# Transposes of q, k and x moved from TensorE to DMA from tile 10 on, with a reordered start and end, in a sliding-window attention and squared-ReLU MLP kernel

## The chip, the cores and the metric

The kernel runs on one core of one Trainium2 chip. The metric is the device time of one execution in microseconds. A core has five engines with in-order instruction streams: TensorE (PE in the profile; its weight loads are listed as PEld), VectorE (DVE), ScalarE (ACT), GpSimd (POOL) and SyncE (SP). SP, ACT and POOL also issue DMAs. An instruction that has to wait holds up everything behind it on its engine.

## The reference

Inputs: q, k, v of shape (4, 8, 768, 64) in fp32 (batch, heads, positions, head size), w_in (512, 2048), w_out (2048, 512); n_global = 8, n_local = 96. Output: (3072, 512) in fp32.

```python
scores = scale * np.matmul(q, k.transpose(0, 1, 3, 2))
rel = pos[:, None] - pos[None, :]
is_global = pos[None, :] < n_global
is_local = (rel >= 0) & (rel < n_local)
dist = np.where(is_global & ~is_local, float(n_local), np.abs(rel))
scores = scores - slopes[:, None, None] * dist          # slopes: one per head
scores = np.where(is_global | is_local, scores, -1e9)
a = softmax(scores)
x = (a @ v).transpose(0, 2, 1, 3).reshape(B * S, H * D)  # (3072, 512)
h = x @ w_in
out = np.maximum(h, 0) ** 2 @ w_out
```

Each position attends to the 96 positions up to itself and to the first 8 positions of its sequence.

## The kernel before

**Tiles and blocks.** The 3072 rows are cut into 24 tiles of 128 (6 for each of 4 batches). A tile goes through attention; two tiles form a block for the MLP, so there are 12 blocks. All matmuls take bf16, except the transposes of tiles 0 and 1, whose q and k come in fp32 by SP and ACT (`plain_q`, `plain_k`, L185). All other loads are issued by POOL (L177) and cast to bf16 on the way.

**Attention of a tile.** PE transposes q and k in four 128x128 blocks each, one per pair of heads (`trq`, `trk`, L327), into PSUM. DVE or ACT copies them out (L264, L266): q into `qz`, in which the two heads of a pair stand in separate halves with zeros between (two copies; the zeros are set at the start, L196), k into `kT`. Four times, once for each pair, PE makes two `sc` matmuls (L375: against the tile's own keys and those of the tile before; the first tile of a batch has only its own), ACT takes exp (L403), and DVE multiplies by `E` (L423), the exponential of mask and slope made once from `pb`. `E0` is the same for the first tile of a batch, where the global keys stand in the tile itself; it is made on ACT from `pb0` (L271). Then in two halves PE multiplies with v (`po`, L466; v has a column of ones, which gives the row sums), and DVE takes the reciprocal and scales into `x` (L491, L492). The first 8 rows of kT and v of each batch are copied into the next tiles (L442, L509), so that two key tiles are enough for each query tile.

**MLP of a block.** PE transposes x (`trx`, L528), a copy puts it into `xT`. Eight steps over d_ff follow: eight `hT` matmuls (L565), relu on ACT (`hr`, L586), square on DVE (`hs`, L598), then two `acc` matmuls (L629) for each of the two row tiles (`sub` 0 and 1), which add up over the eight steps. The sums are copied to `o` and stored by SP (L663).

**What sets the order.** A planner in the kernel (`Plan`) takes the operations with assumed costs, lags and keys, and places at each step the one that can start first, then the one with the lowest key. The result is written out engine by engine; the chip sees only that fixed order and the semaphores. A tile's key lies 12 steps (`LEAD`) ahead of its block's, so attention of later tiles is woven between the MLP steps of earlier blocks. `takes=(ring, n, users)` is a ring of n buffers: `qz` has 4 tiles, `kT` 12, the loaded `q` and `k` 10 each, `x` 2, `xT` 3.

Of the kernel before, what the change touches and what calls it, by code (L numbers as in the profile page):

```python
# [12 lines left out]
FP32 = mybir.dt.float32  # L13
# [84 lines left out]
def kernel(  # L98
# [36 lines left out]
    NQ, NKT, NQZ = 10, 2 * TPB, 4  # L135
# [24 lines left out]
    pb0 = const([P, P], FP32, "pb0")  # L160
    plan = Plan()
    NHS = 14
    LEAD = 12
# [29 lines left out]
    make_identity(nc, ident)  # L193
    nc.vector.tensor_copy(ident32, ident)
    for i in range(NQZ):
        nc.vector.memset(qz[i].bitcast(I32), 0)  # L196
# [12 lines left out]
    nc.vector.tensor_copy(pb0, pb[:, 0, :])  # L209
    nc.vector.tensor_scalar_max(  # L210
        pb0[:n_global, :], pb0[:n_global, :], float(-n_local)
    )
    nc.vector.memset(pb[:n_global, 1, :], float(-n_local))
    for j in range(NT):
        nc.vector.memset(v_sb[j][:, :, D : D + 1], 1.0)  # L215
# [5 lines left out]
    def load_tile(j):  # L221
        q_tile[j], k_tile[j] = q_ring[j % NQ], k_ring[j % NQ]
        for n, dst, src in (("q", q_tile[j], q), ("k", k_tile[j], k)):
# [38 lines left out]
    def any_copy(e, dst, src):  # L262
        if e == "ACT":
            nc.scalar.copy(dst, src)  # L264
        else:
            nc.vector.tensor_copy(dst, src)  # L266

    maskE0 = plan.op(
        ("E0",), {"ACT": 1.6}, key=-99, ready=3.4,
        emit=lambda e: [  # L270
            nc.scalar.activation(E0[:, h // 2, h % 2, :], pb0, Act.Exp, scale=float(slopes[h]))  # L271
            for h in range(H)
        ],
    )
    maskE = [
        plan.op(
            ("E", pair), {"ACT": 0.62}, key=-7 + pair, ready=3.4,
# [9 lines left out]

    tiles = {}
    qz_users = [[] for _ in range(NQZ)]
    kT_users = [[] for _ in range(NKT)]  # L290
    qk_users = [[] for _ in range(NQ)]
    xT_op = {}
# [4 lines left out]
    for j in range(NT):  # L297
# [6 lines left out]
        if j in late:  # L304
            def emit_load(e, j=j):
                load_tile(j)
            ld = plan.op(
                ("load", j), {"POOLQ": 2.6}, emit_load,
                deps=qk_users[j % NQ], key=base, ready=clock[0],
            )  # L310
            qk_users[j % NQ] = []
            land["q", j] = land["k", j] = land["v", j] = ld
# [3 lines left out]
        if True:  # L316
            fp = j < NPLAIN
            parts = []
            for n in ("q", "k"):
                users = []  # L320

                def emit_tr(e, j=j, n=n, fp=fp):
                    pool, tag = (ps_acc, "acc") if fp else (ps_h, "hT")
                    tr = pool.tile([P, NPAIR, P], FP32 if fp else BF16, name=f"tr{n}", tag=tag)
                    src = (q_tile if n == "q" else k_tile)[j]
                    for pair in range(NPAIR):
                        nc.tensor.transpose(  # L327
                            out=tr[:, pair, :], in_=src[:, pair * P : (pair + 1) * P],
                            identity=ident32 if fp else ident,
                        )  # L330
                    tiles["tr", n, j] = tr

                tr = plan.op(
                    ("tr", n, j), {"PE": 0.85 if fp else 0.24}, emit_tr,
                    deps=[land[n, j]], key=base, takes=("acc", NACC, users) if fp else ("hT", 5 - NACC, users),
                )
                users.append(tr)
                if n == "q":
                    for e_ in range(2):
                        half = slice(e_ * D, (e_ + 1) * D)  # L340

                        def emit_z(e, j=j, e_=e_, half=half, zi=zi):
                            any_copy(e, qz[zi][half, :, e_, :], tiles["tr", "q", j][half])

                        z = plan.op(
                            ("z", e_, j), {"DVE": 0.43, "ACT": 0.57}, emit_z,
                            deps=[tr] + qz_users[zi], key=base + 0.1,
                        )
                        users.append(z)
                        parts.append(z)  # L350
                else:
                    def emit_kT(e, j=j, ki=ki):
                        any_copy(e, kT[ki], tiles["tr", "k", j])

                    c = plan.op(
                        ("kT", j), {"DVE": 0.43, "ACT": 0.57}, emit_kT,
                        deps=[tr] + kT_users[ki], key=base + 0.1,
                    )
                    users.append(c)
                    parts.append(c)  # L360
            if not fp:
                qk_users[j % NQ] += [parts[0], parts[-1]]
# [5 lines left out]
        for pair in range(NPAIR):  # L368
            users = []

            def emit_sc(e, j=j, pair=pair, first=first, zi=zi):
                sc = ps_sc.tile([P, 2, 2 * P], FP32, name="sc", tag="sc")
                tiles["sc", j, pair] = sc
                for i in range(1 if first else 2):
                    nc.tensor.matmul(  # L375
                        out=sc[:, i, :],
                        lhsT=kT[(j - i) % NKT][:, pair, :],
                        rhs=qz[zi][:, pair, :, :],
                        start=True,
                        stop=True,  # L380
                        skip_group_check=True,
                    )
# [4 lines left out]
            s_ = plan.op(  # L387
                ("sc", j, pair), {"PE": 0.11 if first else 0.22}, emit_sc, deps=deps,
# [10 lines left out]
            def emit_exp(e, j=j, pair=pair, first=first):  # L399
                n = 2 * P if first else 4 * P  # L400
                esc = work.tile([P, 4 * P], BF16, name="esc", tag="esc", bufs=3)
                sc = tiles.pop(("sc", j, pair))
                nc.scalar.activation(  # L403
                    out=esc[:, :n], in_=sc.rearrange("p a b -> p (a b)")[:, :n],
                    func=Act.Exp, scale=scale,
                )
                tiles["esc", j, pair] = esc

            x_ = plan.op(
                ("exp", j, pair), {"ACT": 0.36 if first else 0.58}, emit_exp, deps=[s_],  # L410
# [6 lines left out]
            def emit_mul(e, j=j, pair=pair, first=first):  # L417
                at = work.tile([P, 4 * P], BF16, name="at", tag="at", bufs=6)
                if first:
                    at_, bias = at[:, : 2 * P], E0[:, pair].rearrange("p b c -> p (b c)")  # L420
                else:
                    at_, bias = at, E[:, pair].rearrange("p i e c -> p (i e c)")
                nc.vector.tensor_mul(  # L423
                    at_, tiles.pop(("esc", j, pair))[:, : at_.shape[1]], bias
                )
                tiles["at", j, pair] = at

            m_ = plan.op(
                ("mul", j, pair), vec(0.24 if first else 0.38), emit_mul,
                deps=[x_, maskE0 if first else maskE[pair]],  # L430
# [4 lines left out]
            mul.append(m_)  # L435
            mul_users.append(musers)
# [18 lines left out]
        for hf in range(2):  # L455
            users = []

            def emit_pv(e, j=j, hf=hf, first=first):
                po = ps_o.tile([P, 4, D + 1], FP32, name="po", tag="po")
                tiles["po", j, hf] = po  # L460
                for hi in range(4):
                    h = 4 * hf + hi
                    at = tiles["at", j, h // 2].rearrange("p (i e c) -> p i e c", i=2, e=2)
                    kjs = (j,) if first else (j, j - 1)
                    for i, kj in enumerate(kjs):
                        nc.tensor.matmul(  # L466
                            out=po[:, hi, :],
                            lhsT=at[:, i, h % 2, :],
# [51 lines left out]
        if True:  # L520
# [26 lines left out]
            xusers.append(f_)  # L547
        xT_op[j] = c
# [64 lines left out]
    for blk in range(NBLK):  # L613
# [7 lines left out]
        for s, sub in order2:  # L621
            users = acc_users[sub]

            def emit_s2(e, blk=blk, s=s, sub=sub):
# [17 lines left out]
                key=8 * blk + s + 2.0, takes=("acc", NACC, users) if s == 0 else None,  # L642
# [3 lines left out]
            if s == NSTEP - 1:  # L646
                ousers = []

                def emit_o(e, blk=blk, sub=sub):
                    o_sb = work.tile([P, d_model], FP32, name="o", tag="o", bufs=4)  # L650
                    any_copy(e, o_sb, tiles.pop(("acc", blk, sub)))
                    tiles["o", blk, sub] = o_sb

                ev = plan.op(
                    ("o", blk, sub), {"ACT": 0.57, "DVE": 0.62}, emit_o,
                    deps=[o], key=8 * blk + s + 1.0, takes=("o", 4, ousers),
                )
                users.append(ev)
                ousers.append(ev)

                def emit_st(e, blk=blk, sub=sub):
                    r0 = (blk * 2 + sub) * P
                    nc.sync.dma_start(out=out[r0 : r0 + P, :], in_=tiles.pop(("o", blk, sub)))  # L663

                st = plan.op(("st", blk, sub), {"SP": 0.4}, emit_st, deps=[ev], key=8 * blk + s + 9.0)
                ousers.append(st)
# [39 lines left out]
```

## Time and profile before

| what | value |
|---|---|
| median of 3 runs (235.57 to 236.24) | 236.1 us |
| profiled execution | 236.87 us |
| its span, first to last instruction | 235.1 us |
| mean granted TensorE clock | 0.997 |
| busy: PE, DVE, ACT, POOL | 93%, 65%, 64%, 31% |
| instructions: PE matmuls, DVE, ACT | 1968, 399, 282 |
| HBM read and written | 27.26 MB and 6.29 MB |

The profile is one execution. Time outside the span (1.77 us) belongs to no instruction. "Busy" is an average over stages that are unlike: a start in which data arrives, a long even middle, and an end in which the last block drains. Rows of groups read: line, engine, operation, out<-in, shapes, count | busy us, mean ns of one | idle time of that engine just before, and what ended it. Rows of the timeline read: start us, length us, engine, line, operation, count, and in brackets the idle time before.

### The profile page before, as it was taken

To read this page: it belongs to the slowest core of one execution; us is meant where nothing else is said; L and a number is where in the kernel's file an instruction comes from. 1 tells how busy PE (TensorE), PEld (TensorE's weight loads), DVE (VectorE), ACT (ScalarE), POOL (GpSimd) and SP (SyncE) were. 2 spreads that over 40 slices of the span, in tenths; PEclk is the share of its full clock that TensorE was granted. 3 is DMA by queue.
4 is the path that set the end of the run, shared out by engine and by line. 5 is a ranking of instruction groups with operands and counts; after the bars stand their busy time and mean duration, and the time that the engine had idled before them with its cause. 6 is when DMAs were issued, how large, how long until landed. Compare 5 with 4: busy or idle time off the path is not lost.

```text
span 235.1 us, 4992 instructions
## 1 busy us (share of the span) xinstructions
PE 219.5 (93%) x1968; PEld 159.1 (68%) x1968; DVE 153.8 (65%) x399; ACT 149.8 (64%) x282; POOL 73.8 (31%) x94
## 2 busy tenths in 40 slices
PE   1768699999999999999999999999999999999992
PEld 1646467866777777777777777777777777776660
DVE  5778466895756866755766766665766676664532
ACT  5778346763686776775776776766776766743341
POOL 6995488797979242143100000000000000000000
PEclk9999999999999999999999999999999999999998
DMA  7999999999999991964900200200200200200202
GB/s 155 138 155 196 180 187 194 157 175 181 203 159 151 193 63 12 156 46 26 158 0 0 92 0 3 89 1 3 89 4 0 92 0 0 92 0 3 89 0 89
DMA packets 84758, 20.76 MB, mean 88 GB/s; under 512 B 75520, under 2 KB 81664, under 8 KB 84736
## 3 DMA queue, kind: packets, MB, share of 16 engines
q0 software_dynamic: 77120, 13.11, 72.0%
q1 hardware_dynamic: 5536, 6.82, 8.4%
q10 hardware_dynamic: 2080, 0.52, 1.2%
q8 instruction: 15, 0.25, 0.4%
q14 instruction: 7, 0.06, 0.1%
HBM read 27.26 MB, written 6.29 MB: 143 GB/s over the span
## 4 chain that ended last, share of the span: by engine, by line
PE 85%; DMA 6%; POOL 3%; DVE 3%; issue 1%; ACT 1%; POOLq 0%
PE hT L565 35%; PE acc L629 33%; PE sc L375 7%; DMA win<-in_moe_w_in_dram 4%; PE po L466 4%; DMA k<-in_k_dram 2%; PE trx L528 2%; PE trk L327 2%; PE trq L327 2%; POOL v L177 2%; DVE qz L196 1%; POOL q L177 1%; DVE x L492 1%; POOL k L177 0%; DVE hs L598 0%
## 5 line engine op out<-in xcount | busy, mean ns | idle before, releaser
L629 PE MATMUL acc<-wout,hs 128*128 128x512 bf16 x384 | 101.1, 379 | 0.8 <-DVE hs L598 0.8
L565 PE MATMUL hT<-xT,win 128*128 128x256 bf16 x768 | 98.4, 273 | 1.9 <-DMA win<-in_moe_w_in_dram 1.9
L586 ACT ACTIVATE hr<-hT 128x512 f32<-128x512 f32 x96 | 57.4, 598 | 62.9 <-PE hT L565 62.6
L565 PEld LDWEIGHTS <-win 128*128 128x128 bf16 x768 | 74.0, 98 | 24.0 <-DMA win<-in_moe_w_in_dram 2.9
L598 DVE TENSOR_TENSOR hs<-hr 128x512 bf16<-128x512 f32 x96 | 65.6, 683 | 27.2 <-ACT hr L586 27.0
L403 ACT ACTIVATE esc<-sc 128x512 bf16<-128x512 f32 (+1 forms) x96 | 52.8, 558 | 5.0 <-PE sc L375 4.4
L629 PEld LDWEIGHTS <-hs 128*128 128x128 bf16 x384 | 34.0, 98 | 21.6 <-DVE hs L598 1.4
L423 DVE TENSOR_TENSOR at<-esc,E 128x512 bf16<-128x512 bf16 (+1 forms) x96 | 37.4, 392 | 0.5 <-ACT esc L403 0.3
L375 PE MATMUL sc<-qz,kT 128*128 128x256 bf16 x176 | 34.5, 277 | 0.2
L177 POOL DMA_DIRECT2D q<-in_q_dram x22 | 19.8, 899 | 28.2 <-PE trk L327 24.3
L491 DVE RECIPROCAL rs<-po 128x4 f32<-128x4 f32 x48 | 8.7, 181 | 30.2 <-PE po L466 29.8
L177 POOL DMA_DIRECT2D v<-in_v_dram x24 | 21.8, 908 | 3.6 <-DVE v L215 1.5
L492 DVE TENSOR_TENSOR x<-po,rs 128x256 bf16<-128x256 f32 x48 | 20.4, 424 | 1.7
L375 PEld LDWEIGHTS <-kT 128*128 128x128 bf16 x176 | 16.9, 99 | 6.0 <-issue 0.3
L177 POOL DMA_DIRECT2D k<-in_k_dram x22 | 19.7, 897 | 2.0 <-DMA q<-in_q_dram 1.0
L466 PE MATMUL po<-v,at 128*128 128x65 bf16 x352 | 19.0, 194 | 1.1 <-DVE x L492 1.1
L466 PEld LDWEIGHTS <-at 128*128 128x128 bf16 x352 | 17.0, 98 | 4.0 <-DVE x L492 1.5
L264 ACT COPY qz<-trq 64x512 bf16<-64x512 bf16 x23 | 13.3, 580 | 5.1 <-DVE qz L266 2.9
L266 DVE COPY qz<-trq 64x512 bf16<-64x512 bf16 x21 | 8.8, 418 | 6.7 <-PE trq L327 5.8
L264 ACT COPY kT<-trk 128x512 bf16<-128x512 bf16 x20 | 11.7, 586 | 1.2 <-PE trk L327 0.7
L264 ACT COPY xT<-trx 128x512 bf16<-128x512 bf16 x17 | 10.0, 589 | 1.3 <-PE trx L528 1.0
L528 PEld LDWEIGHTS <-x 128*128 128x128 bf16 x96 | 7.3, 98 | 4.9 <-DVE x L492 0.4
(39 smaller groups left out, 103.1 us busy)
## 6 DMA issues: line engine op xcount, KB each, us to landing
out_dram<-o SPq DMA_DIRECT2D x24, 256.0 KB, 2.2
v<-in_v_dram POOLq DMA_DIRECT2D x24, 128.0 KB, 6.5
q<-in_q_dram POOLq DMA_DIRECT2D x22, 128.0 KB, 6.4
k<-in_k_dram POOLq DMA_DIRECT2D x22, 128.0 KB, 6.6
win<-in_moe_w_in_dram POOLq DMA_DIRECT2D x8, 256.0 KB, 8.8
wout<-in_moe_w_out_dram POOLq DMA_DIRECT2D x8, 256.0 KB, 8.8
plain_k<-in_k_dram ACTq DMA_DIRECT2D x2, 256.0 KB, 5.4
plain_q<-in_q_dram SPq DMA_DIRECT2D x2, 256.0 KB, 5.0
```

Source lines behind the costliest of these rows:

```text
L177: nc.gpsimd.dma_start(out=dst, in_=src)
L264: nc.scalar.copy(dst, src)
L375: nc.tensor.matmul(out=sc[:, i, :], lhsT=kT[(j - i) % NKT][:, pair, :], rhs=qz[zi][:, pair, :, :], start=True, stop=True, skip_group_check ...
L403: nc.scalar.activation(out=esc[:, :n], in_=sc.rearrange("p a b -> p (a b)")[:, :n], func=Act.Exp, scale=scale,)
L423: nc.vector.tensor_mul(at_, tiles.pop(("esc", j, pair))[:, : at_.shape[1]], bias)
L466: nc.tensor.matmul(out=po[:, hi, :], lhsT=at[:, i, h % 2, :], rhs=v_sb[kj][:, h, :], start=(i == 0), stop=(i == len(kjs) - 1), skip_group_ ...
L492: nc.vector.tensor_tensor(out=x[:, 4 * hf : 4 * hf + 4, :], in0=po[:, :, :D], in1=rs.to_broadcast([P, 4, D]), op=Alu.mult,)
L528: nc.tensor.transpose(out=trx[:, kt, :], in_=x[:, kt * P : (kt + 1) * P], identity=ident)
L565: nc.tensor.matmul(out=hT[:, c, :], lhsT=w_in_sb[s][:, kt, c * P : (c + 1) * P], rhs=tiles["xT", blk][:, kt, :], start=(kt == 0), stop=(kt ...
L586: nc.scalar.activation(hr, tiles.pop(("hT", blk, s)), Act.Relu)
L598: nc.vector.tensor_mul(hs, hr, hr)
L629: nc.tensor.matmul(out=tiles["acc", blk, sub], lhsT=hs[:, c, sub * P : (sub + 1) * P], rhs=w_out_sb[s][:, c, :], start=(s == 0 and c == 0) ...
```

## The change

- From tile 10 on (`JQK`), q and k are no longer transposed on PE. q is loaded by two DMAs (one for the even heads, one for the odd) into `q_pad`, a ring of 8 tiles that already has the zeros between the heads; SP then issues two DMA transposes, `q_pad` to `qz` and `k` to `kT` (operation "T"). POOL zeroes the 8 `q_pad` tiles ahead of tile 10's load.
- From tile 10 on (`JX`), x is transposed by one DMA transpose that SP issues, straight into `xT`.
- Eight matmuls of a tile of zeros stand ahead of the first transpose on PE.
- The ones in v are set ahead of the `qz` zeros on DVE; two of the four `qz` fills come after the mask.
- `E0` is made on DVE from `E`: a copy of its first half, and for the 8 global rows the larger of its two halves.
- In the first tile of a batch, two pairs share one `sc` tile, one exp and one multiplication.
- In the last block, `sub` 1's acc matmuls have a key 50 higher than `sub` 0's, and its last copy and store are made in two halves of 256 columns, one copied by ACT, one by DVE.
- Some of the planner's costs and earliest times (`HOLD`) are changed.

```diff
+    JQK, JX = 10, 10
+    NQ, NPAD, NKT, NQZ = 10, 8, 2 * TPB, 4
+    q_pad = [const([P, NPAIR, 2, P], BF16, f"qpad_{i}") for i in range(NPAD)]
+    NWARM = 8
+    HOLD = {2: 12.5, 3: 15.0}
 make_identity(nc, ident)
+    nc.vector.memset(zero.bitcast(I32), 0)
+    for j in range(NT):
+        nc.vector.memset(v_sb[j][:, :, D : D + 1], 1.0)
...
+    warm = ps_o.tile([P, 4 * P], FP32, name="warm", tag="po")
+    for i in range(NWARM):
+        nc.tensor.matmul(out=warm, lhsT=zero[:, :P], rhs=zero, start=True, stop=True)
...
     def load_tile(j):
+        k_tile[j] = k_ring[j % NQ]
+        todo = [("k", k_tile[j], k)]
+        if j < JQK:
+            q_tile[j] = q_ring[j % NQ]
+            todo.insert(0, ("q", q_tile[j], q))
+        else:
+            q_tile[j] = q_pad[j % NPAD]
+            s_ = src_rows(q, j).rearrange("(a e) p d -> e p a d", e=2)
+            for e in range(2):
+                swdge(("q", j), q_tile[j][:, :, e, e * D : (e + 1) * D], s_[e], 0.43)
...
-    maskE0 = plan.op(
-        ("E0",), {"ACT": 1.6}, key=-99, ready=3.4,
...
+    def emit_E0(e, c):
+        pairs = slice(2 * c, 2 * c + 2)
+        nc.vector.tensor_copy(E0[:, pairs], E[:, pairs, 0])
+        nc.vector.tensor_max(
+            E0[:n_global, pairs], E[:n_global, pairs, 0], E[:n_global, pairs, 1]
+        )
...
             def emit_load(e, j=j):
+                if j == JQK:
+                    for i in range(NPAD):
+                        nc.gpsimd.memset(q_pad[i].bitcast(I32), 0)
                 load_tile(j)
...
+        if j >= JQK:
+            def emit_dT(e, j=j, zi=zi, ki=ki):
+                nc.sync.dma_start_transpose(
+                    out=qz[zi].rearrange("p a b c -> p (a b) c"),
+                    in_=q_tile[j].rearrange("p a b c -> p (a b c)"),
+                )
+                nc.sync.dma_start_transpose(out=kT[ki], in_=k_tile[j])
+            T = plan.op(
+                ("T", j), {"SP": 2.7}, emit_dT,
+                deps=[land["q", j], land["k", j]] + qz_users[zi] + kT_users[ki],
+                key=base - 6,
+            )
...
-        if True:
+        if j < JX:
             users = []
             def emit_f(e, j=j):
...
+        else:
+            def emit_xT(e, j=j, blk=blk, tt=tt):
...
+                nc.sync.dma_start_transpose(
+                    out=tiles["xT", blk][:, :, tt * P : (tt + 1) * P],
+                    in_=tiles["x", j].rearrange("p h d -> p (h d)"),
+                )
+            c = plan.op(("xT", j), {"SP": 1.3}, emit_xT, deps=norm, key=base + 5, takes=xT_ring)
...
-                key=8 * blk + s + 2.0, takes=("acc", NACC, users) if s == 0 else None,
+                key=8 * blk + s + 2.0 + (50 if last and sub else 0),
+                takes=("acc", NACC, users) if s == 0 else None,
...
+                for half in (0, 1) if last and sub == 1 else (None,):
```

How the order changes, at three places. First SP. Before, its whole program is two loads and the 24 stores:

```order
L701 UNCONDITIONAL_BRANCH
L185 DMA plain_q_157<-in_q_dram 128x8x64
L185 DMA plain_q_161<-in_q_dram 128x8x64
L663 DMA out_dram<-o 128x512 x24
L701 UNCONDITIONAL_BRANCH
```

In the changed kernel, from the stores of block 2 on (the number behind qz or kT is its buffer; the first two rows are tile 13's T operation, and the first xT row is tile 10's):

```order
L397 DMA_TRANSPOSE qz_140<-qpad_90 128x8x128
L401 DMA_TRANSPOSE kT_128<-k_96 128x4x128
L397 DMA_TRANSPOSE qz_141<-qpad_91 128x8x128
L401 DMA_TRANSPOSE kT_129<-k_97 128x4x128
L600 DMA_TRANSPOSE xT<-x 128x4x128
L733 DMA out_dram<-o 128x512 x2
L397 DMA_TRANSPOSE qz_142<-qpad_92 128x8x128
L401 DMA_TRANSPOSE kT_130<-k_98 128x4x128
```

Now 42 transposes share SP's stream with the stores: each tile's x stands behind the T operation of a tile four or more later, and two tiles' x and T stand between the stores of two blocks.

Second the end of PE's stream. Before, from the last hT group on, each row standing for a pair of matmuls (acc_3651 is `sub` 0, acc_3657 `sub` 1; the number behind wout is one more than the 143 of step 0 for each step):

```order
L565 MATMUL hT_3734<-xT_3438,win_7_142 128x256
L629 MATMUL acc_3651<-wout_6_149,hs_3730 128x512
L629 MATMUL acc_3657<-wout_6_149,hs_3730 128x512
L629 MATMUL acc_3651<-wout_7_150,hs_3749 128x512
L629 MATMUL acc_3657<-wout_7_150,hs_3749 128x512
```

In the changed kernel (acc_3420 is `sub` 0, acc_3502 `sub` 1; `sub` 1's steps 3 to 7 follow the last row):

```order
L624 MATMUL hT_3487<-xT_3207,win_7_150 128x256
L688 MATMUL acc_3420<-wout_5_156,hs_3481 128x512
L688 MATMUL acc_3502<-wout_0_151,hs_3405 128x512
L688 MATMUL acc_3420<-wout_6_157,hs_3496 128x512
L688 MATMUL acc_3502<-wout_1_152,hs_3423 128x512
L688 MATMUL acc_3502<-wout_2_153,hs_3436 128x512
L688 MATMUL acc_3420<-wout_7_158,hs_3507 128x512
```

`sub` 1's eight steps have moved behind the last hT; before they went step by step with `sub` 0's.

Third the start of DVE's stream, ahead of the first copy from PSUM. Before:

```order
L194 CAST ident_152<-ident 128x128
L196 MEMSET qz_131 128x512
L196 MEMSET qz_132 128x512
L196 MEMSET qz_133 128x512
L196 MEMSET qz_134 128x512
L209 COPY pb_156<-pb 128x128
L210 TENSOR_SCALAR pb_156<-pb_156 8x128
L213 MEMSET pb 8x128
L215 MEMSET v_95 128x8
```

In the changed kernel, from the last of the 24 fills of v on (the zero tile and the other 23 stand ahead):

```order
L200 MEMSET v_126 128x8
L201 CAST ident_160<-ident 128x128
L202 MEMSET qz_139 128x512
L203 MEMSET qz_140 128x512
L216 MEMSET pb 8x128
L217 MEMSET qz_141 128x512
L218 MEMSET qz_142 128x512
```

V's fills, which stood last, now stand first, behind the zero tile alone; the two instructions on pb0 are gone.

More of the change, by code (lines that the diff above doesn't have):

```diff
@@ L286 @@
     ]
+    def emit_E0(e, c):
[4 more added lines that the diff above has]
+        )
+    maskE0 = [
+        plan.op(
+            ("E0", c), {"DVE": 0.6}, emit=lambda e, c=c: emit_E0(e, c), key=-9 + c,
+            deps=maskE[2 * c : 2 * c + 2],
+        )
+        for c in range(2)
+    ]
     tiles = {}
@@ L291 @@
     qk_users = [[] for _ in range(NQ)]
+    pad_users = [[] for _ in range(NPAD)]
     xT_op = {}
@@ L308 @@
                 ("load", j), {"POOLQ": 2.6}, emit_load,
-                deps=qk_users[j % NQ], key=base, ready=clock[0],
+                deps=qk_users[j % NQ] + (pad_users[j % NPAD] if j >= JQK else []),
+                key=base, ready=clock[0],
             )
             qk_users[j % NQ] = []
+            if j >= JQK:
+                pad_users[j % NPAD] = []
             land["q", j] = land["k", j] = land["v", j] = ld
         zi, ki = j % NQZ, j % NKT
-        if True:
[L317 to L335, printed above, removed]
-                )
[L337 to L360, printed above, removed]
-            if not fp:
-                qk_users[j % NQ] += [parts[0], parts[-1]]
@@ new lines, with emit_tr, emit_z, emit_T @@
+        fp = j < NPLAIN
+        parts = []
+        for n in ("q", "k") if j < JQK else ():
+            users = []
+            def emit_tr(e, j=j, n=n, fp=fp):
+                pool, tag = (ps_acc, "acc") if fp else (ps_h, "hT")
+                tr = pool.tile([P, NPAIR, P], FP32 if fp else BF16, name=f"tr{n}", tag=tag)
+                src = (q_tile if n == "q" else k_tile)[j]
+                for pair in range(NPAIR):
+                    nc.tensor.transpose(
+                        out=tr[:, pair, :], in_=src[:, pair * P : (pair + 1) * P],
+                        identity=ident32 if fp else ident,
+                    )
+                tiles["tr", n, j] = tr
+            tr = plan.op(
+                ("tr", n, j), {"PE": 0.85 if fp else 0.24}, emit_tr,
+                deps=[land[n, j]], key=base, ready=HOLD.get(j, 0.0),
+                takes=("acc", NACC, users) if fp else ("hT", 5 - NACC, users),
+            )
+            users.append(tr)
+            if n == "q":
+                for e_ in range(2):
+                    half = slice(e_ * D, (e_ + 1) * D)
+                    def emit_z(e, j=j, e_=e_, half=half, zi=zi):
+                        any_copy(e, qz[zi][half, :, e_, :], tiles["tr", "q", j][half])
+                    z = plan.op(
+                        ("z", e_, j), {"DVE": 0.7 if fp else 0.43, "ACT": 0.57}, emit_z,
+                        deps=[tr] + qz_users[zi], key=base + 0.1,
+                    )
+                    users.append(z)
+                    parts.append(z)
+            else:
+                def emit_T(e, j=j, n=n, ki=ki):
+                    any_copy(e, kT[ki], tiles["tr", n, j])
+                c = plan.op(
+                    ("kT", j), {"DVE": 0.7 if fp else 0.43, "ACT": 0.57}, emit_T,
+                    deps=[tr] + kT_users[ki], key=base + 0.1,
+                )
+                users.append(c)
+                parts.append(c)
+            if not fp:
+                qk_users[j % NQ].append(parts[-1])
@@ L409 @@
             x_ = plan.op(
-                ("exp", j, pair), {"ACT": 0.36 if first else 0.58}, emit_exp, deps=[s_],
+                ("exp", j, pair), {"ACT": 0.58}, emit_exp, deps=[s_],
                 key=base + 0.1 + pair, takes=("esc", 3, eusers),
@@ L418, in emit_mul @@
                 at = work.tile([P, 4 * P], BF16, name="at", tag="at", bufs=6)
[L419 to L422, printed above, removed]
+                bias = E0[:, pair : pair + 2] if first else E[:, pair]
                 nc.vector.tensor_mul(
-                    at_, tiles.pop(("esc", j, pair))[:, : at_.shape[1]], bias
+                    at, tiles.pop(("esc", j, pair)), bias.rearrange("p a b c -> p (a b c)")
                 )
@@ L462, in emit_pv @@
                     h = 4 * hf + hi
-                    at = tiles["at", j, h // 2].rearrange("p (i e c) -> p i e c", i=2, e=2)
+                    pair = h // 2
+                    at = tiles["at", j, pair - pair % 2 if first else pair]
+                    at = at.rearrange("p (i e c) -> p i e c", i=2, e=2)
                     kjs = (j,) if first else (j, j - 1)
@@ L646 @@
             if s == NSTEP - 1:
[L647 to L657, printed above, removed]
```

107 lines of the change are left out of this document (65 added, 42 removed).

## The prediction

> **What bounds the kernel.** I read the page's first two parts, then the stretches, then the chain, then single rows.
>
> ```profile
> span 235.1 us, 4992 instructions
> PE 219.5 (93%) x1968; PEld 159.1 (68%) x1968; DVE 153.8 (65%) x399; ACT 149.8 (64%) x282; POOL 73.8 (31%) x94
> PE   1768699999999999999999999999999999999992
> DMA  7999999999999991964900200200200200200202
> ...
> sum 36.00, PE 25.03 PEld 18.16 DVE 24.54 ACT 22.39 POOL 26.41; mean PE 1.09 PEld 0.79 DVE 1.07 ACT 0.97 POOL 1.15
> ...
> 120.00:200.00 80.00, 80.00 (x745) 58.96 (x744) 53.58 (x135) 56.33 (x104) 0.00 (x0) 1.00 0.08 27
> 228.00:235.00 7.00, 2.48 (x14) 0.98 (x11) 1.39 (x2) 1.18 (x2) 0.00 (x0) 0.89 0.20 75
> ```
>
> The third and fourth lines are the span in 40 slices; the others are stretches (PE, weight load, DVE, ACT, POOL, clock, DMA share, GB/s). PE is idle 10.97 us in the first 36 and 4.52 us in the last 7, and never from 120 to 200, where DVE and ACT are busy 67% and 70%. The middle is bound by PE's instruction stream: a matmul taken out there is time gained, if nothing it feeds comes later. What PE does there:
>
> ```profile
> by line: PE hT L565 39.9%; PE acc L629 38.8%; PE sc L375 9.1%; PE po L466 4.9%; PE trq L327 2.6%; PE trk L327 2.6%; PE trx L528 2.2%
> ...
> 189.17 0.39 PE L327 MATMUL trq<-ident,q 128*128 128x128 bf16 x4
> 189.39 0.39 PE L327 MATMUL trk<-ident,k 128*128 128x128 bf16 x4
> 189.62 1.03 PE L629 MATMUL acc<-wout,hs 128*128 128x512 bf16 x4
> 190.48 1.04 PE L565 MATMUL hT<-xT,win 128*128 128x256 bf16 x8
> ...
> 192.68 0.39 PE L528 MATMUL trx<-ident,x 128*128 128x128 bf16 x4
> 192.90 1.04 PE L565 MATMUL hT<-xT,win 128*128 128x256 bf16 x8
> ...
> 201.65 0.39 PE L528 MATMUL trx<-ident,x 128*128 128x128 bf16 x4
> ```
>
> The first line is the chain from 140 to 200 us: it is PE alone. In the rows, the second number is from the first start to the last end and overlaps what follows; what a piece costs is the distance between starts. Four q transposes cost 0.22 us, four of k 0.23, four of x 0.22, eight hT 0.87, four acc 0.86. A tile takes 8.97 us (192.68 to 201.65).
>
> **Transposes off PE.** Tiles 10 to 23 lose three groups each: 14 x (0.22 + 0.23 + 0.22) = 9.4 us. The 7.4% that the chain gives the three lines (0.66 us of each 8.97) says the same. A tile then needs 8.3 us. Their copies out of PSUM, four a tile, leave DVE and ACT too; those engines had idle time, so I count nothing for it.
>
> In their place stand two SP transposes for q and k, with 256 KB (q with its zeros) and 128 KB read, and one of 128 KB for x: 512 KB in three transfers a tile. No row shows a transpose by DMA. The nearest are the stores, on the same queue, 256 KB each, and the loads:
>
> ```profile
> L663 SPq DMA_DIRECT2D out_dram<-o x24: 332/332/2214, 48.6 to 231.8; - x24
> ...
> DMA to landing us min/median/max: 2.0/2.2/7.4
> ...
> k<-in_k_dram POOLq DMA_DIRECT2D x22, 128.0 KB, 6.6
> ```
>
> An issue takes 0.33 us (2.2 at most); landing takes 2.0 to 7.4 us, median 2.2, and the loads' 6.6 lies inside that. For q and k even 7.4 us is covered: a T operation of tile j needs only the load, and the scores of tile j-4 to have freed the qz buffer, so it can stand two or more tile periods (16 us) ahead of its reader. For x the cover is short, since its transpose starts when the tile is normed and the block's first hT waits for it.
>
> ```profile
> 209.29 0.41 PE L466 MATMUL po<-v,at 128*128 128x65 bf16 x8
> 209.95 0.42 DVE L492 TENSOR_TENSOR x<-po,rs 128x256 bf16<-128x256 f32 x1
> 211.93 1.89 PE L629 MATMUL acc<-wout,hs 128*128 128x512 bf16 x8
> 213.66 1.04 PE L565 MATMUL hT<-xT,win 128*128 128x256 bf16 x8
> 215.39 1.91 PE L565 MATMUL hT<-xT,win 128*128 128x256 bf16 x16
> ```
>
> The po group of 0.24 us ends at 209.53, x is there at 210.37, 0.84 us later; the last block begins at 215.39. In the changed order 24 hT and 14 acc matmuls stand between tile 23's last po and block 11's first hT: 3 x 0.87 + 3.5 x 0.86 = 5.6 us, less 0.84 is 4.8 us of cover. For the six other blocks, counted the same way with their scores, it is 6.5 to 7.0 us, less 0.84: 5.7 to 6.1. Landing between 2.0 and 7.4 plus the issue has its ends on both sides of that. I take 2.2 + 0.33 = 2.5 us, the median, since the x transposes of five of the seven blocks come after about 118 us (slice 21), where the DMA line has fallen to 0 to 2 tenths. One T pair issues ahead of x, but its scores end before the tile's last po, so it has a start of over 2 us. So I cost the moved transposes at nothing, with 7.4 us kept for the rival. Nothing waits longer for x itself: its two buffers come round after two tiles.
>
> On this the Trainium skill speaks with two voices. "VectorE: DVE Perf Modes", section "The three transpose paths", gives 1309 ns to a 128x128 block by the DMA crossbar against 390 ns on TensorE, and its rule is TensorE wherever PSUM will do; the 0.22 us for four here is far less than its TensorE figure. "Advanced Engine Details and Errata", section "X-Bar Transpose (TRN2)", has such DMAs as fast as plain ones, 350 to 400 GB/s. By the second a tile's 512 KB would be an estimated 1.5 us and the sum would stand. By the first, one block after another, it would be an estimated 16 x 1.309 = 20.9 us a tile, and the time an estimated 225.5 + 14 x 12.6 = 402 us. No run here shows either.
>
> **POOL.** Eight zero fills of 128x512 stand ahead of tile 10's load, and each later q load is two issues.
>
> ```profile
> L196 DVE MEMSET qz<- 128x512 int32 x4 | 1.9, 485 | 0.2
> masks.py:197 POOL MEMSET ident<- 128x128 bf16 x1 | 0.2, 205 | 0.3 <-POOLq L687 0.3
> 48.72 0.91 POOL L177 DMA_DIRECT2D q<-in_q_dram  x1
> 109.87 0.88 POOL L177 DMA_DIRECT2D q<-in_q_dram  x1 [5.78 <-PE trk L327]
> ```
>
> A fill is between 0.2 us (the small one) and 1.6 us (the same by bytes): 2 to 13 us in all, and 14 extra issues of up to 0.9 us come to at most 13. Tile 10's load stands at 48.7 us, over 25 us before its scores; later loads wait 5.8 us for their ring. Hidden. Without that cover each 1 us would cost 1 us once.
>
> **The start.** V's ones go ahead of the qz fills, so POOL's first load need not wait for them.
>
> ```profile
> 2.62 0.41 POOL L205 TENSOR_SCALAR_AFFINE_SELECT pb<-pb 128x256 f32<-128x256 f32 x1
> 4.17 0.88 DVE L215 MEMSET v<- 128x8 bf16 x24
> 4.55 1.89 POOL L177 DMA_DIRECT2D v<-in_v_dram  x2 [1.52 <-DVE v L215]
> ...
> 5.00:6.00 1.00, 1.00 (x6) 1.00 (x6) 0.18 (x3) 0.80 (x4) 1.00 (x2) 1.00 1.34 218
> 7.00:8.00 1.00, 0.52 (x3) 0.53 (x4) 0.42 (x1) 0.98 (x4) 1.00 (x2) 1.00 1.81 116
> ...
> 22.26 9.96 DMA win<-in_moe_w_in_dram
> 32.27 1.05 PE hT L565 x8
> ```
>
> The first load can issue 1.52 us sooner. But what ends the start is the fifth w_in slice, 9.96 us in flight, and the DMA line stands at 9 from the second slice on: loads then wait for one another, and those moved up share the engines with q and k of tiles 0 and 1 (218 GB/s). So the gain lies between 0 and 1.5 us. I take 0.4, near the low end, by the full DMA line. The zero matmuls fill time in which PE waits for data (its first slice of 5.9 us is busy at one tenth): eight of acc's shape at 0.86 / 4 are 1.7 us, twice that if PE is slow at first. The mask's eight ACT instructions become four on DVE, and the first tile's scores go two pairs at a time: both lie ahead of the w_in wait. Nothing for these, plus or minus 0.5 us.
>
> **The end.**
>
> ```profile
> 227.55 1.04 PE L565 MATMUL hT<-xT,win 128*128 128x256 bf16 x8
> 228.42 1.03 PE L629 MATMUL acc<-wout,hs 128*128 128x512 bf16 x4
> 230.00 1.04 PE L629 MATMUL acc<-wout,hs 128*128 128x512 bf16 x4 [0.56 <-DVE hs L598]
> 231.08 0.69 DVE L266 COPY o<-acc 128x512 f32<-128x512 f32 x1 [1.13 <-PE acc L629]
> ```
>
> After the last hT, PE has 0.86 us of acc work and then waits 0.6 to 0.7 us for relu and square. Now 22 acc matmuls (4.7 us) follow, those of the last square in their middle, and the wait goes. The last copy, 0.69 us, becomes two halves on two engines, about 0.4 each; a second store issue of 0.33 us takes part of that back. Gain 0.6 + 0.3 = 0.9; ends 0.3 and 1.2.
>
> **Sum.** The profiled execution took 236.87 us around a span of 235.1. 236.87 - 9.4 - 0.4 - 0.9 = 226.2. It lies 0.77 us above the median of 236.1, so the median becomes 225.4, rounded to 225.5. Own range: start to 1.5 and end 1.2 give 224.0; no start gain, a small end and 1 us of scattered waits give 227.5.
>
> **Rivals.**
> Late x (the slower side). The place is the first hT of blocks 5 to 11. If x's transpose lands as slowly as the slowest store, 7.4 + 0.33 = 7.7 us, a block of 5.9 us cover stalls 1.8 us and the last 2.9: 6 x 1.8 + 2.9 = 13.7, so 239.2 us. It decides from 7.4 us on: 10.7 us of gain over seven blocks is 1.5 us each. Against it: that store was one under load, and the median is 2.2. For it: a transpose writes many short pieces, which no row shows. Half as late, 0.5 to 1 us per block, gives 229 to 232.5.
> The queue is full. If transposes run one at a time and each takes 7.4 us, a tile needs 22.2 us against 8.3, and the time is 225.5 + 14 x 13.9 = 420 us. It sets in above 2.8 us per transfer; the store's 2.2 is under that, not by much. The first page named above would have it so.
> The gain is not there: PE's freed time is taken by other waits (DVE or ACT in the chain), and start and end alone are left: 234.8. Against it: both engines shed work.
>
> **Chances.** Forecast 0.68; x half late 0.08; gain not there 0.04; x late 0.13; queue full 0.05; something else slower 0.02. A measurement here tells a change from none at about 0.3%, 0.7 us. Faster: 0.68 + 0.08 + 0.03 = 0.79; same 0.03; slower 0.18. The range goes to the case without gain, 235.0, and down to 223.5, and leaves out the late and full cases, 0.20; the forecast's own is 224.0 to 227.5.
>
> **What the next profile would show.** Right: 168 fewer transposes on PE, tile period 8.3 us after 110 us, PE full there, x's transposes landing in under 4.8 us, no idle before hT put down to xT. Wrong: idle of 1 us or more before a block's first hT, released by a DMA into xT; landing over 6 us; T transposes pushing scores back. At the start, POOL's first load near 3.1 us, with the fifth w_in slice at 31 to 32.3. At the end no idle between the last hT and the last acc.

## The result, and the profile after

The changed kernel takes 228.48 us (median of 4 runs, 227.68 to 230.07) against 236.0 before: a ratio of 0.969, with a 95% interval of 0.964 to 0.975. The time is in the stated range of 223.5 to 235.0, 3 us above the point, but 1 us above the forecast's own 224.0 to 227.5. Two terms of the sum were off, in opposite directions, and one term that I had booked as a gain is none in the changed order.

The page of the changed kernel, parts 1 to 3, the lines that answer to those shown of before:

```profile
span 225.9 us, 4760 instructions
PE 211.8 (94%) x1808; PEld 149.8 (66%) x1808; DVE 150.2 (66%) x379; ACT 123.6 (55%) x226; POOL 86.2 (38%) x116
PE   7488999999999999997699999999999999999992
DMA  7999999999999999999993445454531301301202
q1 hardware_dynamic: 35696, 14.16, 31.6%
```

PE has 160 matmuls fewer (168 transposes gone, 8 zero matmuls added). The PE line has one notch that was not there before, 7 and 6 in the slices from 102 to 113 us. The DMA line stays at 9 until 119 us. Before, it had gaps from 88 us on (slices at 1, 6 and 4 tenths) and was at 0 from 118. Queue 1, which carried 6.8 MB before, carries 14.2, in 30160 packets more: some 240 bytes each, the short pieces that the rival "late x" had in mind.

The notch in rows. First the changed kernel's wait for x, then PE's timeline around it, then SP's queue and DVE ahead of it:

```profile
PE hT L624 <- DMA xT<-x: 3.6, 1, 3.6
...
105.10 0.59 PE L688 MATMUL acc<-wout,hs 128*128 128x512 bf16 x2
109.30 1.05 PE L624 MATMUL hT<-xT,win 128*128 128x256 bf16 x8 [3.60 <-DMA xT<-x]
...
97.03 1.34 SPq L397 DMA_TRANSPOSE qz<-qpad  x1
98.47 1.62 SPq L401 DMA_TRANSPOSE kT<-k  x1
99.41 0.42 DVE L540 TENSOR_TENSOR x<-po,rs 128x256 bf16<-128x256 f32 x1
100.18 2.73 SPq L600 DMA_TRANSPOSE xT<-x  x1
...
100.18 9.08 DMA xT<-x
```

Tile 11's x is there at 99.83, SP issues its transpose at 100.18, and it lands 9.1 us later; block 5's first hT waits 3.6 us. This is the only such stall. Landing times over the run, first of all x transposes, then of those issued in 92 to 93 us (tile 10), 107.5 to 108 (tile 12) and 127.8 to 128 (tile 14):

```profile
DMA to landing us min/median/max: 2.4/2.5/9.1
DMA to landing us min/median/max: 8.3/8.3/8.3
DMA to landing us min/median/max: 7.9/7.9/7.9
DMA to landing us min/median/max: 2.4/2.4/2.4
```

The median of 2.5 us is exactly what I had taken, and it hides what matters: the three that issue while loads are in flight need 7.9 to 9.1 us.

The middle, in SP's rows of two neighbouring tiles' q transposes: a tile takes 8.3 us, as the sum has it.

```profile
125.00 1.23 SPq L397 DMA_TRANSPOSE qz<-qpad  x1
133.31 1.25 SPq L397 DMA_TRANSPOSE qz<-qpad  x1
```

The start, in the changed kernel's timeline, one stretch of 1 us, and the chain up to the fifth w_in slice:

```profile
2.96 1.89 POOL L181 DMA_DIRECT2D v<-in_v_dram  x2
7.00:8.00 1.00, 0.67 (x6) 0.68 (x7) 0.94 (x4) 0.00 (x1) 1.00 (x2) 1.00 2.43 155
19.57 9.80 DMA win<-in_moe_w_in_dram
29.41 1.05 PE hT L624 x8
```

POOL's first load issues at 2.96 instead of 4.55 us, and the fifth slice's hT starts at 29.41 instead of 32.27: 2.9 us, where I had 0.4. In the stretch from 7 to 8 us the DMAs move 155 GB/s instead of 116.

The end, in the changed kernel's timeline:

```profile
216.06 1.04 PE L624 MATMUL hT<-xT,win 128*128 128x256 bf16 x8
216.94 4.91 PE L688 MATMUL acc<-wout,hs 128*128 128x512 bf16 x22
221.89 0.37 ACT L280 COPY o<-acc 128x256 f32<-128x256 f32 x1 [1.57 <-PE acc L688]
222.29 0.42 DVE L282 COPY o<-acc 128x256 f32<-128x256 f32 x1 [3.83 <-ACT o L280]
```

PE's idle time ahead of the last acc matmuls is gone. But the two half copies stand one behind the other: DVE's waits for ACT's.

### The profile page after: what moved, and what is told of

It reads as the page before. It is cut to its first block, busy times and chain, and to the rows that moved or that the text cites. A ratio compares the mean times of both kernels' runs of the same rounds, so it can differ in the third digit from the quotient of the medians.

```text
span 225.9 us, 4760 instructions
## 1 busy us (share of the span) xinstructions
PE 211.8 (94%) x1808; PEld 149.8 (66%) x1808; DVE 150.2 (66%) x379; ACT 123.6 (55%) x226; POOL 86.2 (38%) x116
## 4 chain that ended last, share of the span: by engine, by line
PE 84%; DMA 8%; DVE 4%; ACT 1%; issue 0%; POOL 0%
PE hT L624 35%; PE acc L688 34%; PE sc L425 8%; DMA win<-in_moe_w_in_dram 4%; PE po L514 4%; DMA xT<-x 4%; PE warm L222 2%; DVE qz L282 1%; PE trq L358 1%; PE trx L576 1%; PE trk L358 0%; DVE at L469 0%; ACT qz L280 0%; DVE E L300 0%; POOL v L181 0%
## 5 line engine op out<-in xcount | busy, mean ns | idle before, releaser
L688 PE MATMUL acc<-wout,hs 128*128 128x512 bf16 x384 | 98.8, 379 | 0.2 <-DVE hs L657 0.2
L452 ACT ACTIVATE esc<-sc 128x512 bf16<-128x512 f32 x88 | 51.5, 593 | 3.7 <-PE sc L425 3.7
L469 DVE TENSOR_TENSOR at<-esc,E 128x512 bf16<-128x512 bf16 x88 | 36.3, 416 | 0.8 <-ACT esc L452 0.7
L425 PE MATMUL sc<-qz,kT 128*128 128x256 bf16 x176 | 33.0, 274 | 2.2 <-DVE kT L282 1.6
L181 POOL DMA_DIRECT2D qpad<-in_q_dram x28 | 21.4, 782 | 7.3 <-DMA qz<-qpad 6.1
L282 DVE COPY o<-acc 128x512 f32<-128x512 f32 (+1 forms) x12 | 7.9, 660 | 12.0 <-PE acc L688 8.1
L280 ACT COPY o<-acc 128x512 f32<-128x512 f32 (+1 forms) x13 | 7.4, 569 | 5.5 <-PE acc L688 5.5
L488 DVE COPY kT<-kT 128x32 bf16<-128x32 bf16 x16 | 3.6, 223 | 9.5 <-PE sc L425 9.5
L181 POOL DMA_DIRECT2D q<-in_q_dram x8 | 7.3, 918 | 2.3 <-DMA wout<-in_moe_w_out_dram 1.7
L280 ACT COPY qz<-trq 64x512 bf16<-64x512 bf16 x8 | 4.6, 579 | 4.8 <-DVE qz L282 2.7
```

The source lines that it names most:

```text
L181: nc.gpsimd.dma_start(out=dst, in_=src)
L425: nc.tensor.matmul(out=sc[:, i, :, :], lhsT=kT[kj % NKT][:, p_, :], rhs=qz[zi][:, p_, :, :], start=True, stop=True, skip_group_check=True,)
L452: nc.scalar.activation(out=esc, in_=sc.rearrange("p a b c -> p (a b c)"), func=Act.Exp, scale=scale,)
L469: nc.vector.tensor_mul(at, tiles.pop(("esc", j, pair)), bias.rearrange("p a b c -> p (a b c)"))
L688: nc.tensor.matmul(out=tiles["acc", blk, sub], lhsT=hs[:, c, sub * P : (sub + 1) * P], rhs=w_out_sb[s][:, c, :], start=(s == 0 and c == 0) ...
```

## The experiments

Times are medians, each beside the kernel before on the same chip (235.7 to 236.0).

**x on PE again.**

```diff
-    JQK, JX = 10, 10
+    JQK, JX = 10, 24
```

> x stays on TensorE for all tiles; q and k still go by DMA from tile 10 on. Theory (the one stall of 3.6 us is tile 11's x transpose landing after 9.1 us because it shares the DMA engines with the last loads): the stall goes (-3.6), 14 x 0.22 = 3.1 us of transposes come back, so about 228.0 us, and no idle time of PE over 0.5 us between 40 and 215 us. Rival (the transposes of q and k are what disturbs, in whatever reads them or in the loads behind them): a stall of 2 us or more is still there, at scores or at hT, and the time is 230 or more.

Measured: 227.33 us (ratio 0.964, 0.961 to 0.967), no stall. With 3.1 us more work on PE it is about 1 us faster than the changed kernel: x's transposes by DMA, taken as a whole, cost more than they saved.

**x by DMA from tile 12 on.**

```diff
-    JQK, JX = 10, 10
+    JQK, JX = 10, 12
```

> x goes by DMA from tile 12 on instead of tile 10: block 5's two x transposes are back on TensorE (+0.44 us). Theory (only block 5's x transpose meets the loads): no stall, 228.5 - 3.6 + 0.4 = 225.3 us. Rival (the slow landing is the first x transposes' own, or the load stream reaches one block further): the stall moves to block 6 with 2 us or more, and the time is 227.5 or more.

Measured: 224.47 us (0.952, 0.950 to 0.953), no wait for x; its x transposes land in 2.4 us, 5.3 at most. Two tiles' transposes given back to PE (0.44 us) bring 4.0 us.

**Start and end alone.**

```diff
-    JQK, JX = 10, 10
+    JQK, JX = 24, 24
```

> No transposes by DMA at all: the start and the end of the change alone. Theory (start worth 2.9 us, end 0.7): 236.0 - 3.6 = 232.4 us, and the fifth w_in slice's hT at about 29.4 us as in the changed kernel. Rival (my prediction's terms, 0.4 and 0.9, the remainder coming from the DMA transposes): 234.7 us.

Measured: 233.2 us (0.988, 0.987 to 0.990); hT of the fifth slice at 29.28. By the medians start and end bring 2.8 us; by the two profiled spans (235.1 and 231.5) it is 3.6. The profiled execution of before was 0.8 us above its median, which accounts for the difference. Neither expectation is met to the tenth; the start is worth far more than 0.4. From the fifth slice's hT to the end of the span it takes 202.2 us, against 202.8 before, so some 0.6 us are left for the end in this order.

**No zero matmuls.**

```diff
-    NWARM = 8
+    NWARM = 0
```

> The changed kernel without its eight zero matmuls. Theory (the start is set by the arrival of w_in slices, so the zero matmuls are worth nothing): 228.5 within 0.7 us; the fifth slice's hT within 0.5 us of 29.4; the stretch at 12 to 15 us in which the granted clock was 0.50 is gone or moved. Rival (the zero matmuls bring part of the 2.9 us): 229.5 to 231 us, and the hT later by 1 us or more.

Measured: 228.94 us (0.971, 0.969 to 0.974), hT at 29.23: the zero matmuls bring nothing that shows above the spread. Its profile shows a second effect of the stall, in PE's timeline and in stretches whose column behind POOL is the granted clock:

```profile
108.76 1.05 PE L624 MATMUL hT<-xT,win 128*128 128x256 bf16 x8 [3.22 <-DMA xT<-x]
109.86 1.86 PE L688 MATMUL acc<-wout,hs 128*128 128x512 bf16 x4
111.52 1.91 PE L624 MATMUL hT<-xT,win 128*128 128x256 bf16 x8
...
110.00:111.00 1.00, 1.00 (x4) 0.30 (x2) 0.09 (x1) 0.93 (x2) 0.00 (x0) 0.50 1.60 159
114.00:115.00 1.00, 1.00 (x9) 0.72 (x8) 0.90 (x2) 0.99 (x3) 0.00 (x0) 1.00 2.41 151
```

After PE's 3.2 us without work the granted clock is 0.50 from about 110 to 113 us. From one start to the next, four acc take 1.66 us instead of 0.86 and eight hT 1.70 instead of 0.87: 1.6 us lost on top of the 3.2.

**V's ones last.** On the version with x from tile 12 on.

```diff
-    for j in range(NT):
-        nc.vector.memset(v_sb[j][:, :, D : D + 1], 1.0)
     nc.vector.tensor_copy(ident32, ident)
 ...
     nc.vector.memset(qz[3].bitcast(I32), 0)
+    for j in range(NT):
+        nc.vector.memset(v_sb[j][:, :, D : D + 1], 1.0)
```

> x by DMA from tile 12 on (224.5 us measured) with V's ones put back behind the mask, as the kernel before has them. Theory (the start's 2.9 us come from POOL's first load issuing 1.6 us sooner, and from the loads behind it waiting less): first load at about 4.5 us, the fifth w_in slice's hT near 32 us, time 224.5 + 2.8 = 227.3. Rival (the start's gain comes from the mask on DVE and the paired first tile, which let the tiles ahead of hT finish sooner): hT stays near 29.2 to 30, time 225.3 or less.

Measured: 226.78 us (0.964, 0.961 to 0.967), 2.3 us more than with the ones first. In its timeline:

```profile
4.71 1.90 POOL L181 DMA_DIRECT2D v<-in_v_dram  x2 [1.68 <-DVE v L218]
31.34 1.05 PE L624 MATMUL hT<-xT,win 128*128 128x256 bf16 x8 [0.21 <-DMA win<-in_moe_w_in_dram]
```

The first load is 1.7 us later than with the ones first (2.97), hT of the fifth slice 2.2 us (29.16). The order of 24 small fills makes up most of the start's gain.

**No loads of tiles 16 to 23.** On the changed kernel.

```diff
-                load_tile(j)
+                if j < 16:
+                    load_tile(j)
+                else:
+                    q_tile[j], k_tile[j] = q_pad[j % NPAD], k_ring[j % NQ]
+                    v_sb[j] = v_sb[j - 12]
```

> The changed kernel (x by DMA from tile 10 on) without the loads of tiles 16 to 23, which use older tiles' data, so that the load stream ends some 30 us sooner; all transposes and matmuls stay. Theory (the loads on the same 16 DMA engines make the transposes land late): x's transposes of tiles 10 and 11 land in 2.4 to 4 us instead of 8.3 and 9.1, no stall at block 5's first hT, time 228.5 - 3.6 = 224.9 or some tenths less. Rival (the T pair ahead on SP's queue makes x late): landing stays above 6 us, the stall stays above 2 us, time 227.5 or more.

This kernel leaves out the loads of a third of the tiles and works on older data there. Measured: 223.79 us (0.949, 0.948 to 0.951), no stall. All of its x transposes:

```profile
DMA to landing us min/median/max: 2.4/2.4/3.3
```

The T pair of tile 15 still stands ahead of tile 11's x, which lands in 2.4 us. Without loads beside it the pair costs x nothing.

**Tiles 14 to 16 transposed on PE.**

```diff
+    by_dma = [j >= JQK and j not in (14, 15, 16) for j in range(NT)]
-        if j < JQK:
+        if not by_dma[j]:
```

(and so at the other four places that ask for JQK)

> The changed kernel with tiles 14, 15 and 16 transposed on TensorE again, so that no T pair stands ahead of the x transposes of tiles 10, 11 and 12 on SP; the loads stay, 3 x 0.45 = 1.35 us of PE work come back. Theory (the loads do it): x's transpose of tile 11 still lands after 7 us or more, stall of 2 to 4 us, time 229 to 230. Rival (the T pair does it): landing under 5 us, no stall, time 228.5 - 3.6 + 1.35 = 226.2.

Measured: 225.47 us (0.957, 0.955 to 0.958), no stall, 0.7 us below even the rival's time. The x transposes issued in 99 to 102 us (tile 11) and in 105 to 110 (tile 12):

```profile
L601 SPq DMA_TRANSPOSE xT<-x x1: 1191/1191/1191, 99.7 to 99.7; - x1
DMA to landing us min/median/max: 5.3/5.3/5.3
...
L601 SPq DMA_TRANSPOSE xT<-x x1: 1189/1189/1189, 105.8 to 105.8; - x1
DMA to landing us min/median/max: 3.5/3.5/3.5
```

So my theory that loads alone do it was half right. With loads and T transposes tile 11's x lands after 9.1 us, with loads and without those T pairs after 5.3, with T pairs and without loads after 2.4. The loads are no thinner in this run: from 97 to 105 us POOL issues nine, against four in the changed kernel. The cover of 5.9 us lies between 9.1 and 5.3, so it takes both to pass it. Whether x waits behind the pair on SP's queue, or for DMA engines that the pair and the loads keep busy, is not separated.

**q and k by DMA from tile 8 on.** With x from tile 12 on.

```diff
-    JQK, JX = 10, 10
+    JQK, JX = 8, 12
```

> x by DMA from tile 12 on, and q and k already from tile 8 on: 2 x 0.45 = 0.9 us less on PE than the version at 224.5. Theory (T pairs have a cover of over 16 us, so even landings of 9 us among the loads cost nothing): 223.6 us. Rival (POOL's eight fills now stand ahead of tile 8's load, when loads have less lead, and the longer queue makes scores wait): a wait of PE for qz or kT of 1 us or more, 225 or more.

Measured: 229.54 us (0.974, 0.971 to 0.977), though PE has 0.9 us less to do than at 224.47. The rival's "225 or more" holds, but in the main by other causes:

```profile
PE hT L624 <- DMA xT<-x: 2.9, 1, 2.9
DMA to landing us min/median/max: 2.4/2.5/8.9
DMA  7999999999999999999999925444532301410202
...
39.81 3.81 POOL L334 MEMSET qpad<- 128x512 int32 x8
41.65 2.01 DVE L488 COPY kT<-kT 128x32 bf16<-128x32 bf16 x1
41.92 1.74 DVE L657 TENSOR_TENSOR hs<-hr 128x512 bf16<-128x512 f32 x1
43.72 0.28 PE L425 MATMUL sc<-qz,kT 128*128 128x256 bf16 x1 [1.27 <-DVE at L469]
...
127.00 1.90 PE L688 MATMUL acc<-wout,hs 128*128 128x512 bf16 x4
128.69 1.81 PE L624 MATMUL hT<-xT,win 128*128 128x256 bf16 x8
128.00:129.00 1.00, 1.00 (x5) 0.40 (x3) 0.92 (x2) 0.07 (x1) 0.00 (x0) 0.50 0.82 53
```

The DMA line now stays at 9 until 131 us, two slices longer than in the changed kernel and 24 us past the first x transpose (106.84), and both x transposes of block 6 land after 8.9 us: the stall of 2.9 us is in block 6. Behind it the granted clock is 0.50 from 127 to 130 us, which costs 1.6 us, counted as in the run without zero matmuls. And PE waits 1.3 us for DVE at 43.7: beside POOL's eight fills a kT copy takes 2.01 us (0.18 in the median) and a square 1.74 (0.69), and both end at 43.66, just behind the last fill (43.62). In the changed kernel the same fills, from 45.9 to 49.7 us, stretch no row of DVE; why they do here is open. Together 2.9 + 1.6 + 1.3 - 0.9 = 4.9 of the 5.1 us. The lateness of the T transposes (10.3 us at most) made no score wait; what they do to x does.

**The old end.** With x from tile 12 on, the last block's keys, copy and store as before.

```diff
-                key=8 * blk + s + 2.0 + (50 if last and sub else 0),
+                key=8 * blk + s + 2.0 + 0,
...
-                for half in (0, 1) if last and sub == 1 else (None,):
+                for half in (None,):
```

> The version with x by DMA from tile 12 on (224.5 us measured), its last block's order and last copy and store put back as they were before. Theory (the end is worth 0.7 us, as the distance from the last hT to the end of the span says): 225.2 us, PE idle by 0.5 to 0.7 us ahead of the last acc group. Rival (the end is worth nothing, since the last store's landing sets it): 224.5 within 0.3.

Measured: 224.02 us (0.949, 0.947 to 0.951), the fastest complete version. In the changed order the end part is worth nothing, or costs up to 0.5 us. Its timeline at the end:

```profile
214.56 1.04 PE L624 MATMUL hT<-xT,win 128*128 128x256 bf16 x8
215.43 2.75 PE L688 MATMUL acc<-wout,hs 128*128 128x512 bf16 x12
218.22 0.69 DVE L282 COPY o<-acc 128x512 f32<-128x512 f32 x1 [1.27 <-PE acc L688]
```

Without the transposes the planner weaves the last block in another way: 12 acc matmuls (2.75 us) follow the last hT, enough to cover relu and square, and no idle time is there to take away. And one whole copy (0.69 us) is shorter than two halves in a row.

**No zero matmuls, second time.** With x from tile 12 on.

```diff
-    NWARM = 8
+    NWARM = 0
```

> The same version without the eight zero matmuls. Theory (they are worth nothing here, since the fifth w_in slice ends the start): 224.5 within 0.4 us, hT of the fifth slice at 29.2 within 0.3. Rival (the granted clock of 0.50 that the kernels with zero matmuls showed at 12 to 15 us costs something that the full kernel's stall hid): 223.5 to 224.0.

Measured: 224.43 us (0.951, 0.949 to 0.953) against 224.47. Nothing, in either direction.

## Why the prediction was right, and where it was wrong

The time is in the stated range, but two of the signs that the prediction named for being wrong came: a wait of over 1 us released by a DMA into xT, and landings over 6 us. That the total came within 3 us of the point is in part luck: the start brought about 2.5 us more than booked, against the stall's 3.6 and the end's missing 0.9.

**Transposes off PE, 9.4 us: right.** From start and end alone (233.2) to the kernel whose transposes meet no late loads (223.8) are 9.4 us. The versions with x from tile 12 on and with three tiles on PE give 9.2 and 9.1, with what they give back to PE added. The end's part, some tenths in one order and none in the other, is left inside these differences. The tile period is 8.3 us.

**Moved transposes at nothing: this step failed, for block 5.** The sum took one landing time, the stores' median, for all seven blocks, because five of them come after the loads. For blocks 5 and 6 it gave no reason. The three x transposes issued there by 108 us landed after 7.9 to 9.1 us, more than even the slowest store's 7.4. It also counted the T pair ahead of x as an issue alone, with a start of over 2 us; beside loads the pairs take tile 11's landing from 5.3 to 9.1 us. The cover of 5.7 to 6.1 us was right (5.9 measured), and so was the place of the rival "late x". It happened in one block, not in seven: tiles 10 and 12 are the first of their blocks and have a tile period more, and tile 13's x, at 119.6 us, landed in 3.0. The end of the loads was read rightly from the line of before (118 us, and 119 in the changed kernel), but the gaps that this line had from 88 us on are closed in the changed kernel, with 7.3 MB more on queue 1.

The stall cost 3.6 us in the profiled execution: 223.8 + 3.6 = 227.4 against its 227.68. The median lies 0.8 above that. In two other kernels a stall of 3.2 and 2.9 us was followed by 1.6 us lost to the clock. That the slower executions of the changed kernel have this too is possible but not shown: two of the three have mean clocks (0.977 and 0.975) below every execution of the kernels without the stall (0.981 at least), the third, of 228.57 us, has 0.990. The 0.992 of the profiled execution is a stretch of 0.50 at 12 to 15 us, in the start.

**q and k covered: right.** T transposes landed after up to 9.7 us among the loads, and no score waited for one.

**POOL: right.** The eight fills took 3.8 us together, inside the bounds of 2 to 13, and nothing waited for them in the changed kernel. With q and k by DMA from tile 8 on they cost 1.3 us.

**The start, 0.4 us: mis-sized.** It is 2.9 us by the row of the fifth slice's hT, of which the order of V's fills makes 2.2. I held a DMA line at 9 for a full one. Two stretches of the kernel before, one with V's ones last, and two of POOL's rows before:

```profile
3.00:4.00 1.00, 0.00 (x0) 0.00 (x0) 0.91 (x4) 0.29 (x1) 0.03 (x1) 1.00 1.27 286
7.00:8.00 1.00, 0.52 (x3) 0.53 (x4) 0.42 (x1) 0.98 (x4) 1.00 (x2) 1.00 1.81 116
...
7.00:8.00 1.00, 0.62 (x6) 0.63 (x7) 0.94 (x4) 0.00 (x0) 1.00 (x2) 1.00 1.81 115
...
18.39 0.92 POOL L177 DMA_DIRECT2D q<-in_q_dram  x1 [0.84 <-DMA win<-in_moe_w_in_dram]
19.65 0.88 POOL L177 DMA_DIRECT2D k<-in_k_dram  x1 [0.34 <-DMA wout<-in_moe_w_out_dram]
```

The DMA share (the column before GB/s) does not say what is moved: it is 1.27 at 286 GB/s and 1.81 at 116. Loads moved up by 1.6 us filled the dip at 7 to 8 us (155 GB/s), and with V's ones last it is back. The upper end of 1.5 us was too low too, since the loads behind waited less as well: POOL's two waits of 0.84 and 0.34 us are gone in the changed kernel, and the fifth slice's issue came 2.7 us sooner.

**Zero matmuls and mask at nothing: right** for the zero matmuls (two runs); the mask alone was not tried.

**The end, 0.9 us: wrong.** The first half of it, an idle of 0.6 us, was read in the order of before; there, in the run of start and end alone, about that much is gained, but in the changed order the idle is gone without the edit. The second half, two halves copied at once, did not happen: in the changed kernel DVE's half copy waits for ACT's, and SP issues no store until DVE's half is done (222.71), though ACT's was done at 222.26. Both copies read the same PSUM tile. The Trainium skill, "PSUM — Partial Sum Buffer", section "PSUM bank collisions raise a hardware error", says that two engines must not be in one bank at the same time, reads against reads included. An order of the two copies agrees with that, with 0.37 and 0.42 us one after the other in the trace; that it is the reason for the order is not shown.

**The rival of the full queue: not borne out.** By the 1309 ns a block that the Trainium skill gives ("VectorE: DVE Perf Modes", section "The three transpose paths") the four blocks of x, one after another, would take an estimated 5.2 us; they land in 2.4 us when nothing else runs, and q's eight in 3.1. Nor are the transposes as fast as plain DMAs, as the Trainium skill has them ("Advanced Engine Details and Errata", section "X-Bar Transpose (TRN2)"): q's 256 KB lands in 3.1 us against 2.2 for a store of that size, and an issue on SP takes 1.2 us against 0.33.

## What to carry to other kernels

Work taken off a full PE returned its price here (9.4 us forecast, 9.1 to 9.4 measured). What replaces it has to be priced at the moment when it runs, under the traffic that the change itself adds, and not by the median of a run in which most transfers meet no traffic. For the first blocks that depend on a moved transfer, take the slowest row from the loaded part of the trace; giving two tiles back to PE cost 0.4 us of PE's time here and made the kernel 4.0 us faster. An idle gap at the end belongs to one order: rebuild the order without the edit before booking its removal.

## What was not expected of the hardware

A stall can cost more than its length: after 3.2 us without a matmul the granted clock was 0.50 for 3 us, and so it was after 2.9 us with q and k by DMA from tile 8 on. It does not always follow: in the changed kernel's profile a stall of 3.6 us was followed by a clock of 1.00. The Trainium skill, "TensorE: Matmul & The Clock Gate", section "Why this matters for your kernels", warns of idle gaps over about 3 us between bursts; of the two gaps over 3 us one agrees with that, and the gap of 2.9 us had the same effect without reaching it.

A DMA transpose occupies SP's queue for 1.2 us, and for up to 2.7 in the changed kernel while the DMA line stands at 9, so that a store behind it waits as well: the two stores issued from 94.46 us on had their copies done at 92.3.
